# Pooled attention and experts on one core: the last two head pairs of a batch interleaved by row group, experts scaled and begun per row group, weight decoding in smaller tasks, and a new order

## The chip, the cores and the metric

The kernel runs on one core of a Trainium2 chip. The time is in device microseconds, from start to end of one execution, and a kernel's time is the median of its runs. TensorE is PE in the profile (its weight loads PEld), VectorE DVE, ScalarE ACT, GpSimd POOL, and SyncE, which issues all of this kernel's DMAs, SP.

## The reference

For 4 batches and 8 heads of 1152 keys with 64 values each, neighbouring queries are averaged in pairs (so 576 queries remain), attention is taken over all keys, and the result, 4 x 576 rows of 512 values, goes through two matrices with an exponential unit between them.

```python
q_pool = q.reshape(B, H, S // factor, factor, D).mean(axis=3)
scores = scale * np.matmul(q_pool, k.transpose(0, 1, 3, 2))
attn = softmax(scores)                      # with 1e-09 added to the sum
x = np.matmul(attn, v)                      # heads side by side: 2304 rows of 512
h = x @ w_in                                # 512 -> 2048
g = np.where(h > 0.0, h, np.exp(np.minimum(h, 0.0)) - 1.0)
return g @ w_out                            # 2048 -> 512
```

(The softmax is shortened here.) Everything is float32; the weights reach the kernel as 64-bit words, as the code's views of two 32-bit words show.

## The kernel before

**Arithmetic.** Every operand of a matmul is split into two float16 parts, a high half (the value scaled and rounded) and a low half (what is left). A product is then three matmuls or their equivalent. Making a low half is one VectorE instruction with two inputs in SBUF (`lo`, `plo`), or two instructions on POOL (a scaling and a subtraction).

**Attention.** Work goes batch by batch. A batch has 4 head pairs, and a pair has 9 steps: 4 tiles of 128 queries for each of its two heads, and one step with the last 64 queries of both. That is 144 steps in all. One step is: scores on PE (L643, L649) into the single PSUM buffer `s`; the maximum over the keys, which also moves the scores to SBUF, on DVE (L655); the exponential on ACT (L661), its sum (L666) and the reciprocal (L669); the high half of the probabilities on POOL (L672) or ACT (L680); the low half on DVE (L675), or, in the steps that the code calls slow, a scaling and a subtraction on POOL (L683 or L686 on ACT, L689); and a transposing DMA into `pT` (L699). Two steps share one product with the values on PE (L736, L742); ACT and DVE bring it into `x32` (L754, L759). The buffer `ep` holds a step's scores and probabilities from the maximum until the transpose has landed. There are 3 of these; batch 0 may also use the memory that w_out fills later (buffer names `wo`), and its `pT` the memory of `x16`.

**Before a pair begins**, `prep` loads q, k and v, adds the query pairs, finds the largest values by sums (L346), scales by them, makes the halves (L351 and L363 on ACT and DVE, or L306 and L369 on POOL), transposes keys and queries by DMA (L451, L439) and copies parts of the queries' transpose (L445, L448). `kT`, `qT` and `v16` have two buffers each.

**Weights.** `weights` loads each of 8 groups of both matrices in two halves, decodes the 64-bit words to float32 on DVE (L520, L524, L529), sums their sizes on ACT (L537), and makes halves once the scale is known (`split`: L574, L577, or L306 and L583 on POOL). Groups of w_in are scaled one by one, w_out as a whole.

**Experts.** When a batch's attention is complete, its largest value is found (L786, L793, then a turn on PE, L319 to L326), its rows are scaled into `x16` (L821 on ACT, L826 on DVE), and then come two row groups, rows 0 to 255 and rows 256 to 575: first matrix on PE (L850), the unit in five instructions on ACT, POOL and DVE (L858, L861, L866, L871, and the halves L885 to L897), and the second matrix on PE (L917, 12 matmuls a task), with the result scaled and written out (L928 to L938). `x16` has one buffer, and so has `x32`.

**What sets the order.** Nothing is scheduled on the chip. Each piece of work is a task with an engine, an assumed duration, a due time (`key`), what it follows, and the buffers that it uses; some have a second way on another engine. `Plan.run` places them one after another, on each free engine the ready task with the earliest due time whose buffers are free, and takes the second way where that ends sooner by its assumed durations (`WIN`, `PEN`). The instructions are then written in that order, and every engine runs its own in order. Due times are those of a step (`t0`, which advances by T0 or T1) shifted by a constant for each kind of work, all in `CFG`.

## Time and profile before

| | us |
|---|---|
| median of 3 runs | 980.82 |
| lowest and highest run | 978.5 and 980.83 |
| the profiled execution | 977.62 |
| its span, first to last instruction | 975.8 |
| PE busy | 745.6 (76%) |
| DVE busy | 747.6 (77%) |
| ACT busy | 627.9 (64%) |
| POOL busy | 519.0 (53%) |

No engine is busy all of the time; the shares are averages over stretches that differ. So the rows to look at are those by stretch, then the waits inside each, then single instructions in order of time. A row of instructions gives the line, the engine, the operation, what is written from what, shapes and count; behind the bar the busy time, the mean time of one in ns, and the idle time of the engine just before them with what ended it.

### The profile page before, as it was taken

Reading aid. Unit: us, or ns where it says so; the run is one execution under the profiler, and the core shown is the slowest. Engines: PE = TensorE matmul, PEld = TensorE weight load, DVE = VectorE, ACT = ScalarE, POOL = GpSimd, SP = SyncE. Lnnn points to the kernel's source line nnn. Section 1 sums busy time; section 2 is a strip of 40 time slices with the busy share of each in tenths; the row PEclk is TensorE's granted clock in tenths of the full one; section 3 lists DMA queues with packets and bytes.
Section 4 is the critical chain, followed back from the end, with each engine's and each line's share of the span. In section 5 each row is a group of like instructions: output and inputs, shape, how many; then the busy total and the mean of one; then the engine's idle time right before and its main releaser. Section 6 shows DMA issues by size and latency. Waiting matters only on the chain.

```text
span 975.8 us, 14669 instructions
## 1 busy us (share of the span) xinstructions
PE 745.6 (76%) x5271; PEld 416.6 (43%) x5271; DVE 747.6 (77%) x1200; ACT 627.9 (64%) x1093; POOL 519.0 (53%) x422
## 2 busy tenths in 40 slices
PE   0364464654258989889769997989698999999997
PEld 0122132322126645544346444544365455458563
DVE  5797989899789978788778776887877789845150
ACT  3576786666476868776557666865677778734260
POOL 4373867477579963783247634771276247505130
PEclk9998575556659999999979998999799999999999
DMA  7599899899956989999977989799888698640000
GB/s 238 134 212 228 190 199 254 184 227 222 271 109 126 177 156 184 171 177 184 183 148 137 206 163 193 132 203 190 172 174 172 132 176 135 123 94 7 22 2 27
DMA packets 434057, 156.94 MB, mean 161 GB/s; under 512 B 395840, under 2 KB 414272, under 8 KB 433984
## 3 DMA queue, kind: packets, MB, share of 16 engines
q1 hardware_dynamic: 433984, 156.01, 78.6%
q8 instruction: 41, 0.67, 0.3%
q14 instruction: 32, 0.26, 0.1%
HBM read 45.09 MB, written 4.72 MB: 51 GB/s over the span
## 4 chain that ended last, share of the span: by engine, by line
PE 32%; DMA 21%; DVE 12%; POOL 6%; issue 2%; ACT 2%; SPq 2%; DVEq 0%; POOLq 0%; ACTq 0%
DMA pT<-ep 16%; PE r L917 12%; PE r L850 8%; DVE ep L655 5%; PE r L736 4%; PE s L643 3%; DVE ep L675 3%; PE r L742 2%; PE s L649 2%; DMA kT<-kn 2%; DMA qT<-qn 1%; DMA q<-in_q_dram 1%; POOL ep L672 1%; ACT ep L661 1%; DVE tmp L871 1%
## 5 line engine op out<-in xcount | busy, mean ns | idle before, releaser
L655 DVE TENSOR_SCALAR_CACHE_REDUCE ep<-s,sm 128x1152 f32<-128x1152 f32 x133 | 188.0, 1414 | 80.1 <-DMA pT<-ep 52.2
L661 ACT ACTIVATE ep<-ep,nm 128x1152 f32<-128x1152 f32 x133 | 166.5, 1252 | 98.7 <-DVE ep L655 86.1
L850 PE MATMUL r<-x,wi 128*128 128x256 f16 (+1 forms) x1536 | 201.9, 290 | 9.3 <-DVE x L759 3.1
L643 PE MATMUL s<-kT,qT 128*128 128x512 f16 (+3 forms) x480 | 122.3, 370 | 113.1 <-DVE ep L655 88.9
L675 DVE SCALAR_TENSOR_TENSOR ep<-ep,nm 128x1152 f16<-128x1152 f32 x118 | 193.5, 1642 | 9.2 <-POOL ep L672 6.3
L917 PE MATMUL r<-wo,g 128*128 128x512 f16 (+1 forms) x864 | 174.8, 380 | 0.5 <-DVE tmp L871 0.3
L850 PEld LDWEIGHTS <-wi 128*128 128x128 f16 x1536 | 148.1, 99 | 60.1 <-issue 18.4
L736 PE MATMUL r<-pT,v 128*128 128x256 f16 (+1 forms) x864 | 100.8, 268 | 61.7 <-DMA pT<-ep 49.4
L672 POOL TENSOR_SCALAR ep<-ep,nm 128x1152 f16<-128x1152 f32 x52 | 73.2, 1408 | 104.2 <-DVE nm L669 102.5
L866 POOL TENSOR_SCALAR tmp<-tmp,us 128x320 f32<-128x320 f32 (+1 forms) x96 | 79.6, 830 | 90.4 <-ACT tmp L861 85.6
L680 ACT ACTIVATE ep<-ep,nm 128x1152 f16<-128x1152 f32 x81 | 101.3, 1251 | 31.0 <-DVE nm L669 30.7
L643 PEld LDWEIGHTS <-qT 128*128 128x128 f16 (+1 forms) x480 | 44.8, 106 | 174.8 <-issue 135.3
L917 PEld LDWEIGHTS <-g 128*128 128x128 f16 (+1 forms) x864 | 73.1, 100 | 88.9 <-issue 9.3
L736 PEld LDWEIGHTS <-v 128*128 128x128 f16 x864 | 68.8, 105 | 93.6 <-issue 47.7
L871 DVE SCALAR_TENSOR_TENSOR tmp<-r,wk,tmp 128x320 f32<-128x320 f32 (+1 forms) x96 | 58.0, 611 | 33.4 <-POOL tmp L866 33.2
L649 PE MATMUL s<-kT,qT 64*128 64x512 f16 (+3 forms) x480 | 80.8, 370 | 0.0
L754 ACT ACTIVATE x<-r,sm 64x256 f32<-64x256 f32 (+1 forms) x96 | 39.9, 415 | 47.3 <-PE r L742 45.4
L893 POOL TENSOR_SCALAR g<-tmp 128x320 f16<-128x320 f32 (+1 forms) x55 | 46.7, 850 | 35.8 <-DVE tmp L871 33.4
L742 PE MATMUL r<-pT,v 128*64 128x256 f16 (+1 forms) x864 | 65.5, 274 | 0.0
L858 ACT ACTIVATE tmp<-r 128x320 f32<-128x320 f32 (+1 forms) x96 | 46.3, 484 | 26.5 <-PE r L850 25.0
L889 POOL TENSOR_TENSOR g<-tmp,g 128x320 f16<-128x320 f32 (+1 forms) x54 | 56.8, 1058 | 4.8 <-ACT g L885 3.0
L861 ACT ACTIVATE tmp<-tmp,us 128x320 f32<-128x320 f32 (+1 forms) x96 | 57.7, 609 | 1.5
(136 smaller groups left out, 1029.2 us busy)
## 6 DMA issues: line engine op xcount, KB each, us to landing
k<-in_k_dram SPq DMA_DIRECT2D x16, 576.0 KB, 4.9
v<-in_v_dram SPq DMA_DIRECT2D x16, 576.0 KB, 4.9
q<-in_q_dram SPq DMA_DIRECT2D x32, 256.0 KB, 3.4
qT<-qT SPq DMA_DIRECT2D x48, 144.0 KB, 2.8
g<-in_moe_w_in_dram SPq DMA_DIRECT2D x13, 512.0 KB, 5.4
g<-in_moe_w_out_dram SPq DMA_DIRECT2D x13, 512.0 KB, 4.8
out_dram<-tmp SPq DMA_DIRECT2D x16, 256.0 KB, 2.5
pT<-ep SPq DMA_TRANSPOSE x133, 4.8
```

The costliest lines, as they stand in the source:

```text
L643: nc.tensor.matmul(s.ap[rows, c, 0:n], pr.qT.ap[:, 0, j, rows], keys[c], start=True, stop=False, skip_group_check=True,)
L649: nc.tensor.matmul(s.ap[rows, c, 0:n], pr.qT.ap[r, 1, j, rows], keys[c][r], start=False, stop=True, skip_group_check=True,)
L655: nc.vector.tensor_scalar(e_(), s.ap.rearrange("p a b -> p (a b)")[:, 0:S], pr.sm.ap[:, 12:13], None, op0=ALU.mult, op1=ALU.min, accum_out ...
L661: nc.scalar.activation(out=e_(), in_=e_(), func=AF.Exp, bias=nm.ap[:, 0:1], scale=-1.0, accum_out=nm.ap[:, 2:3],)
L672: nc.gpsimd.tensor_scalar(p_(0), e_(), nm.ap[:, 3:4], 1.0, op0=ALU.mult, op1=ALU.mult)
L675: nc.vector.scalar_tensor_tensor(out=p_(1), in0=e_(), scalar=nm.ap[:, 3:4], in1=p_(0), op0=ALU.mult, op1=ALU.subtract)
L680: nc.scalar.activation(out=p_(0), in_=e_(), func=AF.Copy, scale=nm.ap[:, 3:4])
L736: nc.tensor.matmul(x.ap[:, os], vt[:, order[c]].rearrange("p e d -> p (e d)"), pT.ap[:, c, cs], start=(c == 0), stop=False, skip_group_che ...
L742: nc.tensor.matmul(x.ap[r0:r0 + 64, os], vt[:, order[c], 0], pT.ap[:, NCH + c, cs], start=False, stop=(c >= NCH - 2), skip_group_check=True,)
L850: nc.tensor.matmul(hp.ap[:, f * n:(f + 1) * n], w[:, a, c, (f0 + f) * 128:(f0 + f + 1) * 128], x16.ap[:, e, c, g0:g0 + n], start=(i == 0), ...
L866: nc.gpsimd.tensor_scalar(en.ap[:, :m], en.ap[:, :m], -1.0, us.ap[:, 5:6], op0=ALU.add, op1=ALU.mult)
L917: nc.tensor.matmul(op.ap[r0:r0 + tn, :], gt[qd].ap[:, a, fi, o:o + tn], w_out16(f // 2)[:, e, f % 2, :], start=(i < 128 // tn), stop=(i >= ...
```

## The change

**Order of the steps.** The first two pairs of a batch keep their order. The last two are interleaved: the tiles 0 and 1 of both heads of pair 2, the same of pair 3, then the rest of pair 2 and the rest of pair 3. With the first half of this, rows 0 to 255 of the batch are complete; the time of it is kept in `u.ready`.

**Experts by row group.** `experts` is called once for each row group, with a start of its own. Each call finds the largest value of its own rows, scales them, and has its own scaling words (`us`, now 3 buffers); `x16` is shared by both calls of a batch.

**Weight decoding.** One task for two halves of a group becomes a task for each half, which waits for its own load alone, and also for the keys' low half of the very first pair (`first_keys`).

**Order made anew.** The constants are other ones, many of them apart for batch 0 (`K`); slow steps are every second of batch 0 as before, and every ninth after it (two in 36 to 39 before, and none behind that). The window in which a pair is prepared is set by PA and PB. `wm` has one buffer instead of two.

```diff
-            jobs = [(h, t) for h in range(2) for t in range(u.nt)] + ([(None, u.nt)] if u.lo else [])
+            mine.append(pr)
+        early = [(h, t) for h in range(2) for t in range(2)]
+        late_ = [(h, t) for h in range(2) for t in range(2, u.nt)] + [(None, u.nt)]
+        turns = [(pr, early + late_) for pr in mine[:-2]] + [(pr, early) for pr in mine[-2:]] + [(pr, late_) for pr in mine[-2:]]
+        for pr, jobs in turns:
...
+            if pr is mine[-1]:
+                u.ready.append(now)
...
-            prep(pr, prev.t0 - 2000.0, pr.t0 - 4000.0)
+            prep(pr, prev.t0 - CFG["PA"], pr.t0 - CFG["PB"])
+    first_keys = pairs[0].kl
...
-        td = plan.add("DVE", 4700.0, t0, dec, lds, raws + us + to)
-        tm = plan.add("ACT", 2 * act(512) + 260.0, t0, osum, [td], raws + us + to + wm)
+            td = plan.add("DVE", 2450.0, t0 + s, dec, [lds[s], first_keys], [raws[s], us[s]] + to)
+            tms.append(plan.add("ACT", act(512) + 130.0, t0 + s, osum, [td], [raws[s], us[s]] + to + wm))
...
-        slow = st.i < CFG["NS"] and st.i % PLM == PLM - 1
+        every = K("PLM", u)
+        slow = every and st.i % every == every - 1 and (u.i > 0 or st.i < CFG["NS0"])
...
-    def experts(u, t0, t1):
-        us, x16 = plan.buf("us"), plan.buf("x16")
+    def experts(u, gi, t0, t1):
+        us, x16 = plan.buf("us"), u.x16
+        g0, n = u.groups[gi]
...
-                    us.ap[:, to:to + 1], u.x32.ap[:, p0:p1, :u.n], axis=AX.XY, op=ALU.max, apply_absolute_value=True
+                    us.ap[:, to:to + 1], u.x32.ap[:, p0:p1, g0:g0 + n], axis=AX.XY, op=ALU.max, apply_absolute_value=True
...
-        if u.i + 1 < len(units):
-            experts(u, u.t1 + CFG["M0"], units[u.i + 1].t1 + CFG["M1"])
-        else:
-            experts(u, u.t1 + CFG["M0"], u.t1 + 100000.0)
+        u.x16 = plan.buf("x16")
+        ends = units[u.i + 1].ready if u.i + 1 < len(units) else [u.t1 + 100000.0, u.t1 + 200000.0]
+        experts(u, 0, u.ready[0] + CFG["M0"], u.ready[1] + CFG["M2"])
+        experts(u, 1, u.ready[1] + CFG["M2"], ends[0] + CFG["M1"])
```

The constants (`CFG`) are one line of numbers for another and are not shown. What they do to the order is shown at three places; a name there is a tile, and line numbers behind the change are its own.

The first is DVE at the start of the program, right behind the scaling words of the first pair (`sm`). `h` and `g` hold raw weights, `tmp` a decoder's scratch, and `qn`, `kn` and `v` the low halves of the first pair's queries, keys and values. Before:

```order
L306 TENSOR_SCALAR sm_94<-sm_94 128x1
L432 TENSOR_SCALAR sm_94<-sm_94 128x1
L520 TENSOR_SCALAR tmp_119<-h_91 128x512
L520 TENSOR_SCALAR tmp_120<-g_98 128x512
L524 SCALAR_TENSOR_TENSOR tmp_119<-h_91,tmp_119 128x512
L524 SCALAR_TENSOR_TENSOR tmp_120<-g_98,tmp_120 128x512
L529 SCALAR_TENSOR_TENSOR h_91<-h_91,tmp_119 128x512
L529 SCALAR_TENSOR_TENSOR g_98<-g_98,tmp_120 128x512
L363 SCALAR_TENSOR_TENSOR kn_96<-k_86,sm_94,kn_96 128x9x64 x2
```

After, at the same place:

```order
L324 TENSOR_SCALAR sm_94<-sm_94 128x1
L450 TENSOR_SCALAR sm_94<-sm_94 128x1
L381 SCALAR_TENSOR_TENSOR qn_93<-q_81,sm_94,qn_93 128x9x64
L381 SCALAR_TENSOR_TENSOR kn_96<-k_86,sm_94,kn_96 128x9x64 x2
L381 SCALAR_TENSOR_TENSOR v_123<-v_88,sm_94,v_123 128x18x64
L541 TENSOR_SCALAR tmp_136<-h_91 128x512
L542 SCALAR_TENSOR_TENSOR tmp_136<-h_91,tmp_136 128x512
L545 SCALAR_TENSOR_TENSOR h_91<-h_91,tmp_136 128x512
```

The keys' low halves stand ahead of the decoding instead of behind two halves of it, and the low halves of queries and values, which POOL made before, stand on DVE beside them.

The second is where the halves of w_out are made, at the change from batch 0 to batch 1. Before, on POOL (L306 and L583 on `wo` are one low half; L683, L689 and L672 belong to attention steps):

```order
L306 TENSOR_SCALAR wo_1325<-wo_1325,wk 128x512
L583 TENSOR_TENSOR wo_1325<-wo_1325 128x512
L689 TENSOR_TENSOR ep_1882<-ep_1882 128x1152
L306 TENSOR_SCALAR wo_1409<-wo_1409,wk 128x512
L583 TENSOR_TENSOR wo_1325<-wo_1409,wo_1325 128x512
L306 TENSOR_SCALAR wo_1409<-wo_1409,wk 128x512
L583 TENSOR_TENSOR wo_1325<-wo_1409,wo_1325 128x512
L683 TENSOR_SCALAR ep_1940<-ep_1940,nm_1939 128x1152
```

After, on DVE (L591 on `wo` is one low half, L669 a maximum, L689 a low half of probabilities):

```order
L591 SCALAR_TENSOR_TENSOR wo_1751<-wo_1751,wk 128x512 x2
L381 SCALAR_TENSOR_TENSOR v_2187<-v_1875,sm_1499,v_2187 128x18x64
L591 SCALAR_TENSOR_TENSOR wo_1751<-wo_1566,wk,wo_1751 128x512 x2
L689 SCALAR_TENSOR_TENSOR ep_2032<-ep_2032,nm_2031 128x1152
L591 SCALAR_TENSOR_TENSOR wo_1566<-wo_1566,wk 128x512 x2
L669 TENSOR_SCALAR ep_2277,nm_2276<-s_2178,sm_1130 128x1152
L591 SCALAR_TENSOR_TENSOR wo_1566<-wo_1320,wk,wo_1566 128x512 x2
L689 SCALAR_TENSOR_TENSOR ep_2127<-ep_2127,nm_2126 128x1152
L683 RECIPROCAL nm_2276<-nm_2276 128x1
L591 SCALAR_TENSOR_TENSOR wo_1320<-wo_1320,wk 128x512 x2
```

All 16 low halves of w_out stand on DVE after the change, where 6 stood on DVE and 10 on POOL.

The third is ACT in the last batch (`x_6424` is `x32`, `x_8313` is `x16`; L661 is a step's exponential, L754 an attention result, L928 an output). Before:

```order
L754 ACTIVATE x_6424<-r_8114,sm_6687 64x256
L661 ACTIVATE ep_8134,nm_8133<-ep_8134,nm_8133 128x1152
L666 ACTIVATE nm_8133<-nm_8133,wk 128x1
L928 ACTIVATE tmp_8166<-r_7973,us_5834 128x512
L754 ACTIVATE x_6424<-r_8171,sm_6687 64x256
L754 ACTIVATE x_6424<-r_8219,sm_6687 64x64 x2
L928 ACTIVATE tmp_8276<-r_8080,us_5834 128x512
L821 ACTIVATE x_8313<-x_6424,us_8060 128x4x256
L821 ACTIVATE x_8313<-x_6424,us_8060 128x4x320
```

After (L836 scales rows into `x16`, L675 is an exponential, L694 a high half of probabilities, L769 an attention result, L873 and L876 begin an expert tile's unit):

```order
L836 ACTIVATE x_8117<-x_6774,us_7932 128x4x256
L675 ACTIVATE ep_8115,nm_8114<-ep_8115,nm_8114 128x1152
L769 ACTIVATE x_6774<-r_8087,sm_6682 64x256
L680 ACTIVATE nm_8114<-nm_8114,wk 128x1
L694 ACTIVATE ep_8115<-ep_8115,nm_8114 128x1152
L873 ACTIVATE tmp_8192<-r_8132 128x512
L876 ACTIVATE tmp_8192<-tmp_8192,us_7932 128x512
L675 ACTIVATE ep_8164,nm_8163<-ep_8164,nm_8163 128x1152
...
L769 ACTIVATE x_6774<-r_8615,sm_7251 64x64 x2
L943 ACTIVATE tmp_8707<-r_8556,us_7932 128x512
L836 ACTIVATE x_8117<-x_6774,us_8438 128x4x320
```

The scaling of rows 0 to 255 and the units of their experts stand among the last steps, with six exponentials behind that scaling; only the 320 rows are scaled behind the last attention result.

## Rows read from the trace of the kernel before

**Rows 1.** Busy time by stretch: start:end, length, engines' busy us (count), PEclk, DMA share, GB/s

```profile
37.20:322.00 284.80, 155.84 (x956) 79.83 (x957) 255.99 (x420) 190.56 (x332) 194.94 (x112) 0.71 0.91 197
188.80:253.50 64.70, 33.42 (x191) 16.27 (x191) 59.66 (x94) 37.04 (x69) 40.97 (x23) 0.63 1.05 236
322.00:817.00 495.00, 433.79 (x3239) 245.20 (x3238) 399.18 (x626) 351.69 (x610) 263.43 (x238) 0.96 0.89 170
870.00:976.00 106.00, 100.86 (x674) 62.05 (x672) 34.53 (x65) 39.62 (x71) 24.28 (x35) 1.00 0.05 16
```

(The engines stand in the order PE, PEld, DVE, ACT, POOL.)

**Rows 2.** Waits of DVE, 322 to 817 us: total us, times, longest

```profile
DVE ep L655 <- DMA pT<-ep: 41.5, 32, 5.0
```

**Rows 3.** Timeline of PE from 868 us: start, us, what, count

```profile
869.30 0.34 PE L742 MATMUL r<-pT,v 128*64 128x64 f16 x9
...
876.81 21.17 PE L850 MATMUL r<-x,wi 128*128 128x256 f16 x192
897.82 5.34 PE L917 MATMUL r<-wo,h 128*128 128x512 f16 x24
903.00 15.70 PE L917 MATMUL r<-wo,g 128*128 128x512 f16 x72
918.54 26.30 PE L850 MATMUL r<-x,wi 128*128 128x320 f16 x192
944.67 26.18 PE L917 MATMUL r<-wo,g 128*128 128x512 f16 x144
```

**Rows 4.** Timeline of the start: DVE, SP's queue (SPq) and PE

```profile
13.87 1.39 DVE L520 TENSOR_SCALAR tmp<-h 128x512 uint32<-128x512 uint32 x1
...
20.41 4.78 DVE L363 SCALAR_TENSOR_TENSOR kn<-k,sm,kn 128x576 f16<-128x576 f32 x2
...
27.43 5.06 SPq L451 DMA_TRANSPOSE kT<-kn  x1
...
35.38 1.12 PE L643 MATMUL s<-kT,qT 128*128 128x512 f16 x3 [6.60 <-DMA qT<-qT]
```

**Rows 5.** Groups of instructions over the whole run, shapes kept apart

```profile
L675 DVE SCALAR_TENSOR_TENSOR ep<-ep,nm 128x1152 f16<-128x1152 f32 x118 | 193.5, 1642 | 9.2 <-POOL ep L672 6.3 <-ACT ep L680 2.6
L363 DVE SCALAR_TENSOR_TENSOR kn<-k,sm,kn 128x576 f16<-128x576 f32 x26 | 29.3, 1166 | 0.0
L369 POOL TENSOR_TENSOR v<-v,v 128x1152 f16<-128x1152 f32 x10 | 27.8, 2777 | 0.8
L871 DVE SCALAR_TENSOR_TENSOR tmp<-r,wk,tmp 128x512 f32<-128x512 f32 x32 | 23.8, 744 | 10.2 <-POOL tmp L866 10.0
L306 POOL TENSOR_SCALAR v<-v,sm 128x1152 f32<-128x1152 f32 x10 | 16.7, 1672 | 1.0 <-ACT v L351 0.6
L306 POOL TENSOR_SCALAR wo<-wo,wk 128x512 f32<-128x512 f32 x9 | 11.4, 1266 | 0.3 <-ACT wo L574 0.3
L577 DVE SCALAR_TENSOR_TENSOR wi<-g,wk,wi 128x512 f16<-128x512 f32 x11 | 10.3, 960 | 0.0
L363 DVE SCALAR_TENSOR_TENSOR v<-v,sm,v 128x1152 f16<-128x1152 f32 x6 | 9.3, 1546 | 1.9 <-POOL v L306 1.9
L363 DVE SCALAR_TENSOR_TENSOR qn<-q,sm,qn 128x576 f16<-128x576 f32 x5 | 5.5, 1104 | 0.0
```

**Rows 6.** A group of 37 to 322 us, and one line's shortest, median and longest ns

```profile
L675 DVE SCALAR_TENSOR_TENSOR ep<-ep,nm 128x1152 f16<-128x1152 f32 x18 | 37.7, 2093 | 0.1
...
L524 DVE SCALAR_TENSOR_TENSOR tmp<-g,tmp x26: 671/684/2847, 16.6 to 267.8; 128x512 uint32<-128x512 uint32 x26
```

**Rows 7.** A group of 37 to 322 us: idle time ahead of the maximum, and releasers

```profile
L655 DVE TENSOR_SCALAR_CACHE_REDUCE ep<-s,sm 128x1152 f32<-128x1152 f32 x34 | 48.0, 1411 | 18.7 <-PE s L649 9.5 <-DMA pT<-ep 8.6
```

**Rows 8.** DMA issues: count, us from issue to landing (median)

```profile
pT<-ep SPq DMA_TRANSPOSE x133, 4.8
qT<-qn SPq DMA_TRANSPOSE x16, 3.8
kT<-kn SPq DMA_TRANSPOSE x16, 5.8
```

127 lines of the change are left out of this document (65 added, 62 removed).

## Prediction

> **What bounds the kernel now.** I read the busy time by stretch first, then who waits, and last the single instructions at both ends of the program. The stretches [rows 1] cut the run at the 1st, 46th and 136th row maximum on VectorE (L655, one for each of the 144 attention steps) and at the end of the last attention product. Three different limits show. From 37 to 322 us (steps 1 to 45) DVE is busy 256.0 of 284.8 us, 90%, while PE is at 55% and its granted clock averages 0.71, so part of the stretch runs at 1.2 GHz and part at 2.4: DVE is the limit. From 322 to 817 us (steps 46 to 135) PE is busy 433.8 of 495 us (88%) and DVE 399.2 (81%); neither is full, and the longest wait of DVE there is for a transposed tile, 41.5 us [rows 2]: three `ep` buffers, each held until its transpose has landed, tie the engines together. After 870 us PE alone works: 100.9 of 106 us. In [rows 3] this tail is seen in a row: the last attention product at 869.30, some left-over expert work, then all of the last batch's experts, 21.2 + 5.3 + 15.7 + 26.3 + 26.2 us, with nothing beside them.
>
> The profiled execution took 977.6 us, 1.8 over its span of 975.8; the median of the three runs is 980.8, 3.2 above it. I make the sum as a difference against the profiled run and put it on the median.
>
> **The change, term by term.**
>
> *End.* With the last two pairs interleaved, rows 0 to 255 of the last batch are complete while steps are left. In the new order PE begins their experts behind the scores of step 140 of 144, and behind the last attention product stand 6 tasks of 12 output matmuls, then the 320-row experts. Now: 869.64 to 970.85 us, 101.2 us. After: 6 x 2.62 (15.70 / 72 x 12) + 26.3 + 26.2 = 68.2 us [rows 3], and a wait. The chain that must finish behind those six tasks (evacuation, maximum, turn, scaling) ran from 869.64 to 876.81 in the kernel before, 7.2 us with matmuls over it; the six tasks give it 15.7 us, but the return matmul stands only one task from the end of them, so I add 1.5 us for the two scaling instructions that follow it. That is 69.7, a gain of 31.5 us. Bounds: 24 (the chain is not covered) and 36 (part of the six tasks slips ahead of the last product). I take **-31**.
>
> *Start.* DVE now decodes two weight halves from 13.87 us, 6.5 us long, before the keys' low halves at 20.41; these take 4.8 us beside POOL, the next loads of k and v wait for them, and the transpose of the keys, issued at 27.43, occupies its queue for 5.06 us; the first scores follow at 35.38 [rows 4]. The new order puts low halves of q, k and v ahead of the decoding: 0.8 to 1.1 + 1.6 to 4.8 + 1.4 to 2.2 us, so keys are done 3 to 7 us sooner. But on SP the k and v loads now stand ahead of both transposes, and the row at 27.43 shows a transpose that sits in the queue while loads are under way, so about half is lost. **-3**, from -6 to +3.
>
> *Steps 1 to 45, the dear one.* Batch 0's experts start behind the scores of step 33 instead of 41, and the planner chose DVE over POOL more often. Counted in the order ahead of the 46th maximum, DVE gets 12 more low halves of w_out (x 0.960 = 11.5), 6 more of the keys (x 1.166 = 7.0), 4 more of v (x 1.546 = 6.2), 2 more of the probabilities (x 1.642 = 3.3), 7 more joins (x 0.744 = 5.2, a little high since 3 are narrower) [rows 5], and some 6 us of small ones (an estimate: two subtractions, a weight half, ten one-column instructions). Together +39 us on the engine that is the limit. POOL loses 5 pairs for v (1.672 + 2.777), 7 for w_out (two of 1.266) and 3 for keys (taken like those for v), about 53 us [rows 5], and 9 normalisations, and gets about 25 us of expert work earlier: net -40 of 195 us.
>
> That matters to DVE. The low half of the probabilities takes 2093 ns on average in this stretch against 1642 over the run [rows 5], and one and the same decode instruction ranges from 671 to 2847 ns with a median of 684 [rows 6]. Each group's time less its count times its shortest instruction, summed over this stretch's DVE groups (an estimate), is 50 us beside 195 us of POOL [rows 1], 0.26 us for each. So -40 of POOL gives back 10, and DVE's demand grows by 29 us.
>
> The Trainium skill's page "SBUF — State Buffer", section "Who interferes with whom", goes further: VectorE and GpSimd share a port pair by an exclusive lock, and the second to start waits until the first is done. The single worst rows agree (2847 against 671 ns); the mean, 0.26 us lost for one us of POOL, does not, since POOL mostly meets other instructions. By the rule taken in full, this term would be about -1 instead.
>
> Of the 29 us, what goes into DVE's idle 28.8 us? 9.5 us of it are waits for scores and 8.6 for transposes [rows 7]. The first should shrink, since earlier experts keep PE at the higher clock; in the densest piece, 188.8 to 253.5 us, DVE reached 92% [rows 1]. I take 13 us, a little under half of the idle time, as filled: **+16**. Bounds: +9 (DVE at 97%: 285 / 0.97 = 294) and +43 (39 us with no relief, at 90% busy).
>
> *Steps 46 to 135.* DVE loses 10 low halves of the probabilities (-16.4), which every ninth step now gives to ACT and POOL, and gets 4 for v (+6.2), 4 for q (+4.4), and about 8 us of scaling and subtractions, since each batch is scaled twice: +2. POOL is 36 us lighter, so DVE nets about -4 (36 x 0.16, this stretch's rate worked out in the same way, is 6). PE gets 15 us more expert work by the order. PE has 61 us of idle time here, DVE 96, and neither is full, so I let the two cancel: **0**. Bounds: -15 (DVE's waits for transposes, 41.5 us, fall by a third as steps follow each other more evenly) and +25 (PE's 15 as they are, and 10 for the mechanism of rival C).
>
> *Steps 136 to 144* keep their 53 us: PE loses 10 us of left-over experts, and DVE gets 12 of the new group's joins. The second buffer `wm` that is taken away (a scaling word of the weights) can delay a decode only behind the previous group's scaling; it lies in the second term.
>
> Sum: -31 - 3 + 16 + 0 = **-18**: 980.8 - 18 = 963 us.
>
> **Rivals.**
>
> *A, POOL was the brake.* If each us of POOL that goes was one that DVE waited for, the 40 us come back whole and the first 45 steps cost nothing (39 - 40). For it: the 2093 ns mean [rows 6]. Against: 0.26. -31 - 3 - 1 = -35: 980.8 - 35 = 946 us.
>
> *B, the first 45 steps stay bound by DVE and pay in full.* The place is the 285 us before the experts' main part; price +43, as above, because the idle time there is latency that the new order keeps. For it: 90% busy over all of the stretch, and 0.1 us of idle time ahead of the low halves [rows 6]. Against: POOL does get lighter. -31 - 3 + 43 = +9: 990 us, slower than before. It decides from +34 on, where it eats the whole gain of the two ends.
>
> *C, turnover of buffers.* kT, qT and v16 have two buffers each. Interleaved, the last two pairs hold both of each; pair 3 begins 4 steps after pair 2 (9 before), and the next batch's first pair has 5 steps between the release and its own scores. Into these must go transposes of 3.8 and 5.8 us and the copies that follow them, in one queue with the steps' own transposes of 4.8 us [rows 8]. Eight such turns at 2.5 us each: +20, so -18 + 20 = +2: 983 us, no change. Against: 4 steps are 22 us at 5.5 us a step, and no wait of PE for these tiles past the start is among the longer ones today.
>
> *D, it does not do what it says*: PE is in order, and an expert task placed too early would stall the scores behind it. It would look like C in time, and I give it no chance of its own.
>
> **How the numbers follow.** Forecast 0.42, A 0.20, B 0.24, C 0.14. The forecast's own range, from its middle bounds, is 948 to 978. A reaches down to 938 with the lower bound of steps 46 to 135 partly drawn; B reaches up to 994. Range 938 to 994. What a measurement of this kernel can tell from no change is 0.3%, 3 us. Faster: nearly all of the forecast and A, and a little of C: 0.64. Same: the forecast's edge and half of C: 0.10. Slower: B and the rest of C: 0.26.
>
> **What would show it.** End: from the last attention product to PE's end about 70 us, not 101. Start: first maximum near 34 us. First 45 steps: about 300 us long, DVE above 92%, the low halves' mean under 2.0 us; B would show 325 us, A 285 with means near 1.6. Steps 46 to 135: 495 us, PE above 90%; C would show waits of scores for kT or qT. The forecast is wrong if steps 46 to 135 move by more than 20 us either way, which no row here excludes.

## The result, and the profile after

The changed kernel takes 994.8 us (median; 993.0 to 998.7), 1.0148 times the kernel before, 95% interval 1.0109 to 1.0186: slower by 1.5%, clear of noise though under 2%. The forecast was 963 us, its range 938 to 994. The profiled execution spans 993.3 us, against 975.8 before. The first view to read is the busy time by stretch, cut at the 1st, 46th and 136th maximum (L669 now) and at the end of the last attention product. It answers [rows 1]. The columns are start:end, length, busy time of PE, PE weight loads, DVE, ACT and POOL, granted TensorE clock, DMA share and GB/s:

```profile
34.30:344.40 310.10, 198.17 (x1181) 102.52 (x1181) 279.46 (x471) 213.96 (x366) 143.74 (x93) 0.75 0.85 183
344.40:860.90 516.50, 441.89 (x3237) 247.52 (x3237) 396.18 (x653) 365.38 (x622) 230.48 (x215) 0.95 0.84 164
860.90:919.50 58.60, 52.96 (x442) 35.19 (x442) 38.91 (x66) 41.55 (x64) 24.98 (x22) 0.88 0.65 113
919.50:993.30 73.80, 68.41 (x411) 37.97 (x410) 20.78 (x47) 26.35 (x52) 11.63 (x20) 1.00 0.05 17
```

| stretch | before | after | difference | predicted |
|---|---|---|---|---|
| to the first maximum | 37.2 | 34.3 | -2.9 | -3 |
| steps 1 to 45 | 285.0 | 310.2 | +25.2 | +16 |
| steps 46 to 135 | 494.5 | 516.4 | +21.9 | 0 |
| steps 136 to the last product's end | 53.0 | 58.6 | +5.6 | 0 |
| from there to the end | 106.2 | 73.8 | -32.4 | -31 |
| span | 975.8 | 993.3 | +17.5 | -18 |

(The cut for steps 1 to 45 lies at 344.42.) Both ends of the program came out as forecast; the middle lost more than they gained.

Summed over steps 46 to 135, neither PE (442 us, 433 before) nor DVE (396, 399 before) has much more to do; in the sum, what grew is waiting. The sum hides where it happens. The stretch holds the first two pairs of batches 2 and 3 (steps 73 to 90 and 109 to 126). These take 24.9 us more, with 24.8 us more work on DVE and 23.7 on PE. The other steps have 27.3 us less work on DVE and are only 2.9 us shorter (288.1 for 291.0). The sums of the two windows of first pairs, before and after:

```profile
sum 203.46, PE 172.21 PEld 100.30 DVE 158.30 ACT 138.87 POOL 89.31; mean PE 86.11 PEld 50.15 DVE 79.15 ACT 69.44 POOL 44.66
sum 228.33, PE 195.95 PEld 108.73 DVE 183.06 ACT 164.40 POOL 122.86; mean PE 97.98 PEld 54.37 DVE 91.53 ACT 82.20 POOL 61.43
```

DVE's waits in all of steps 46 to 135, to be read against [rows 2] (what waits <- for what: us in total, times, longest):

```profile
DVE ep L669 <- DMA pT<-ep: 52.1, 32, 4.2
DVE nm L683 <- ACT nm L680: 20.1, 28, 2.2
DVE ep L689 <- POOL ep L686: 10.5, 9, 1.4
...
DVE x L774 <- ACT x L769: 9.1, 12, 1.8
```

PE's tail, beside [rows 3]: the last attention product (L757) ends at 919.47, six tasks of 12 output matmuls follow, and behind them the 320-row experts. PE waits 0.37 us in all of it for the scaled rows (L841). Columns: start, duration, instruction, count, idle time before it:

```profile
919.13 0.34 PE L757 MATMUL r<-pT,v 128*64 128x64 f16 x9
919.40 2.76 PE L932 MATMUL r<-wo,g 128*128 128x512 f16 x12
922.00 2.75 PE L932 MATMUL r<-wo,h 128*128 128x512 f16 x12
924.60 5.34 PE L932 MATMUL r<-wo,g 128*128 128x512 f16 x24
...
936.55 25.70 PE L865 MATMUL r<-x,wi 128*128 128x320 f16 x188 [0.37 <-DVE x L841]
962.09 26.18 PE L932 MATMUL r<-wo,g 128*128 128x512 f16 x144
```

The start, beside [rows 4]: the keys' low halves are done at 17.3 us, before any decoding, but their transpose is issued only at 21.84, behind two loads and the queries' transpose, and stands in its queue for 4.59 us. Its issue is 5.6 us earlier than in [rows 4], the first maximum 2.9, so half of the lead was lost, as the prediction had assumed. In both kernels the first scores wait last for a copy of the queries' transpose (`qT<-qT`, L466 now), which stands behind both transposes in the queue; it is issued 2.7 us earlier (30.01 for 32.74):

```profile
15.79 1.54 DVE L381 SCALAR_TENSOR_TENSOR kn<-k,sm,kn 128x576 f16<-128x576 f32 x2
...
19.20 2.57 SPq L457 DMA_TRANSPOSE qT<-qn  x1
...
21.84 4.59 SPq L469 DMA_TRANSPOSE kT<-kn  x1
...
30.01 0.46 SPq L466 DMA_DIRECT2D qT<-qT  x1
...
32.46 1.12 PE L657 MATMUL s<-kT,qT 128*128 128x512 f16 x3 [0.79 <-DMA qT<-qT]
...
34.27 1.42 DVE L669 TENSOR_SCALAR_CACHE_REDUCE ep<-s,sm 128x1152 f32<-128x1152 f32 x1 [5.08 <-PE s L663]
```

### The profile page after: what moved, and what is told of

It is laid out like the page before. It is cut to its first block, busy times and chain, and to the rows that moved or that the text cites. A ratio compares the mean times of both kernels' runs of the same rounds, so it can differ in the third digit from the quotient of the medians.

```text
span 993.3 us, 14724 instructions
## 1 busy us (share of the span) xinstructions
PE 765.5 (77%) x5283; PEld 425.0 (43%) x5283; DVE 751.7 (76%) x1269; ACT 658.6 (66%) x1122; POOL 414.4 (42%) x357
## 4 chain that ended last, share of the span: by engine, by line
PE 34%; DMA 18%; DVE 14%; POOL 6%; issue 4%; ACT 3%; SPq 1%; DVEq 0%; POOLq 0%; ACTq 0%
DMA pT<-ep 16%; PE r L932 13%; PE r L865 7%; DVE ep L669 5%; PE r L751 4%; PE s L657 4%; PE s L663 3%; PE r L757 2%; DVE ep L689 2%; DMA q<-in_q_dram 1%; POOL tmp L881 1%; ACT ep L675 1%; POOL g L904 1%; DVE tmp L886 1%; DVE tmp L542 1%
## 5 line engine op out<-in xcount | busy, mean ns | idle before, releaser
L669 DVE TENSOR_SCALAR_CACHE_REDUCE ep<-s,sm 128x1152 f32<-128x1152 f32 x136 | 192.1, 1413 | 76.3 <-DMA pT<-ep 57.1
L675 ACT ACTIVATE ep<-ep,nm 128x1152 f32<-128x1152 f32 x136 | 170.2, 1251 | 102.1 <-DVE ep L669 93.2
L865 PE MATMUL r<-x,wi 128*128 128x256 f16 (+1 forms) x1536 | 199.4, 288 | 2.6 <-DVE tmp L886 1.4
L932 PE MATMUL r<-wo,g 128*128 128x512 f16 (+1 forms) x888 | 182.5, 383 | 2.2 <-DVE tmp L886 2.2
L689 DVE SCALAR_TENSOR_TENSOR ep<-ep,nm 128x1152 f16<-128x1152 f32 x110 | 165.1, 1501 | 15.2 <-POOL ep L686 11.9
L865 PEld LDWEIGHTS <-wi 128*128 128x128 f16 x1536 | 147.5, 98 | 49.8 <-issue 11.2
L694 ACT ACTIVATE ep<-ep,nm 128x1152 f16<-128x1152 f32 x95 | 118.8, 1250 | 28.5 <-DVE nm L683 28.0
L751 PE MATMUL r<-pT,v 128*128 128x256 f16 (+1 forms) x846 | 106.5, 281 | 33.6 <-DMA pT<-ep 24.8
L881 POOL TENSOR_SCALAR tmp<-tmp,us 128x320 f32<-128x320 f32 (+1 forms) x96 | 75.1, 784 | 103.1 <-ACT tmp L876 98.4
L932 PEld LDWEIGHTS <-g 128*128 128x128 f16 (+1 forms) x888 | 77.3, 101 | 92.1 <-issue 9.6
L686 POOL TENSOR_SCALAR ep<-ep,nm 128x1152 f16<-128x1152 f32 x41 | 53.2, 1298 | 141.4 <-DVE nm L683 139.8
L703 POOL TENSOR_TENSOR ep<-ep 128x1152 f16<-128x1152 f32 x26 | 67.8, 2607 | 55.5 <-ACT ep L700 49.2
L904 POOL TENSOR_TENSOR g<-tmp,g 128x320 f16<-128x320 f32 (+1 forms) x54 | 62.4, 1162 | 16.9 <-ACT g L900 16.0
L769 ACT ACTIVATE x<-r,sm 64x256 f32<-64x256 f32 (+1 forms) x96 | 39.9, 416 | 41.0 <-PE r L757 39.7
L757 PE MATMUL r<-pT,v 128*64 128x256 f16 (+1 forms) x846 | 65.1, 277 | 0.0
L873 ACT ACTIVATE tmp<-r 128x320 f32<-128x320 f32 (+1 forms) x96 | 46.5, 484 | 23.7 <-PE r L865 19.2
L876 ACT ACTIVATE tmp<-tmp,us 128x320 f32<-128x320 f32 (+1 forms) x96 | 57.1, 609 | 1.5
```

What stands on the lines that cost most here:

```text
L669: nc.vector.tensor_scalar(e_(), s.ap.rearrange("p a b -> p (a b)")[:, 0:S], pr.sm.ap[:, 12:13], None, op0=ALU.mult, op1=ALU.min, accum_out ...
L675: nc.scalar.activation(out=e_(), in_=e_(), func=AF.Exp, bias=nm.ap[:, 0:1], scale=-1.0, accum_out=nm.ap[:, 2:3],)
L689: nc.vector.scalar_tensor_tensor(out=p_(1), in0=e_(), scalar=nm.ap[:, 3:4], in1=p_(0), op0=ALU.mult, op1=ALU.subtract)
L694: nc.scalar.activation(out=p_(0), in_=e_(), func=AF.Copy, scale=nm.ap[:, 3:4])
L751: nc.tensor.matmul(x.ap[:, os], vt[:, order[c]].rearrange("p e d -> p (e d)"), pT.ap[:, c, cs], start=(c == 0), stop=False, skip_group_che ...
L757: nc.tensor.matmul(x.ap[r0:r0 + 64, os], vt[:, order[c], 0], pT.ap[:, NCH + c, cs], start=False, stop=(c >= NCH - 2), skip_group_check=True,)
```

## The experiments

Two questions were open: why steps 46 to 135 grew, and what the first 45 steps paid for. The ratio of each kernel below is to the kernel before, with its 95% interval; the times of stretches come from one profiled execution each. Single profiles differ: i2 below keeps DVE's order of before up to the 61st maximum, and still its steps 1 to 45 took 288.3 us instead of 285.0. So a difference of 3 us in a stretch is no finding.

### Which part of the change: constants, slow steps, halves, last batch

**e1, the changed code with the constants of before** (`us` with two buffers).

```diff
-    LOADS=70959, ..., KM=-3090, KE=104873, ..., KE0=162320, ..., PLM=9, M2=13636, ..., PB=12759,
+    LOADS=39538, PLM=0, ..., KM=7701, KE=39223, ..., KE0=39223, ..., PB=4000, M2=32900
```

> The changed code with the constants of the kernel before (the slow steps of batch 0 alone, the old windows, the old pacing of the experts moved 22.8 us of due time ahead for the earlier start). Theory 1: the 22 us lost in steps 46 to 135 come from the structure, the interleaving and the two scalings a batch; then this run loses them too (about 515 us there) and ends near 990. Theory 2: they come from the new constants (every ninth step slow, other due times); then steps 46 to 135 take about 495 us here and the whole is near 970. In both the last product to the end should be near 74 us, since the tail hangs on the structure alone, and the first 45 steps show whether the extra DVE work there is the planner's choice under the new constants (then 285 us) or the earlier experts' (then 305).

Measured 1006.2 us, 1.0278 [1.0241, 1.0314]. Steps 1 to 45 take 290.0 us, steps 46 to 135 535.3, the rest 142.8. So all but 5 us of the 25 lost in the first 45 steps come with the new constants, which begin batch 0's experts sooner; what they buy is at the end (132.4 instead of 142.8) and in between (516 instead of 535). Over steps 1 to 135 the two kernels take the same time, 825.3 and 826.6 us: the constants move the loss and do not make it. The tail behind the last attention product is 87.2 us here, not the 74 expected, so it does not hang on the structure alone.

**e5, no slow steps behind batch 0**: in the order of the changed kernel, POOL's and ACT's part of them is an ordinary low half on DVE.

```diff
+        if slow and u.i > 0:
+            norm_pool = norm_act = lambda: None
+            plo_pool = plo
```

> The changed kernel in its own order, with one edit: the slow steps of batches 1 to 3 (every ninth) make their low half by one VectorE instruction at the place where POOL's subtraction stood, and the normalisation on ACT or POOL is dropped. Theory 2a: the slow steps hold an ep buffer longer and cost the waits that grew (POOL's high half, 4.9 to 10.5 us; the transposes, 41.5 to 52.1); then steps 46 to 135 shrink by 10 us or more. Rival: they relieve DVE as meant; then the stretch grows by up to 14 us, 10 times 1.4. If neither binds there, within 3 us.

Measured 997.1 us, 1.0185 [1.0110, 1.0261]; steps 46 to 135 take 516.1 us (516.4 with them). In this stretch the slow steps neither cost nor help.

**e6, low halves given back to POOL**, all but one instruction of them in the first 45 steps: 10 of w_out, 5 of v, 3 of keys, at their place in the changed order. (The cut shows w_out alone.)

```diff
+            if which and (g, s) not in ((0, 0), (1, 0), (2, 0), (4, 0), (5, 0), (7, 0)):
+                t.back = lo_pool
```

> The changed kernel in its own order, with 10 low halves of w_out, 5 of v and 3 of the keys in batches 0 and 1 given back to POOL at the same places, as the kernel before had them. If DVE's added instructions are what makes the first 45 steps 25 us longer, these 18 (about 10 x 0.96 + 5 x 1.55 + 3 x 2.33 = 24 us, less 10 for POOL's interference) shorten the stretch from 310 by about 14 us. If POOL's interference weighs as much as the instructions themselves, or the earlier experts and not these halves are the cost, nothing is gained, or it grows.

Measured 1012.2 us, 1.0339 [1.0297, 1.0381]. Steps 1 to 45, the first of its windows here, are 14 us longer, though DVE does 6 us less in them:

```profile
35.20:359.30 324.10, 196.81 (x1181) 101.22 (x1182) 273.14 (x451) 214.17 (x366) 186.86 (x127) 0.76 0.80 175
```

The expected gain did not come. At this place in the order the halves are better on DVE. What DVE's added work costs by itself this run can't tell, since POOL became 43 us busier and other work waits for it.

**e3, the kernel before with only the last batch interleaved and done by row group**, and the experts of the batch before it paced 22.8 us of due time faster, to make room.

```diff
+        if u.i == B - 1:
+            turns = [(pr, plain) for pr in mine[:-2]] + [(pr, early) for pr in mine[-2:]] + [(pr, late_) for pr in mine[-2:]]
```

> The kernel before with one part of the change and only in the last batch: its last two pairs interleaved, its two row groups scaled and begun apart, and the experts of the batch before it paced 22.8 us of due time faster to make room. If the tail is won by that alone, the last product to the end is 74 us against 106, and what the faster pacing costs shows in steps 100 to 144: at no cost the whole ends near 950, if PE has to pay for each us of expert work that is moved ahead of the last product (some 30 us), near 980.

Measured 989.6 us, 1.0108 [1.0079, 1.0137]. The tail is as short as in the changed kernel, but the nine steps ahead of it take 85.4 us instead of 53.0:

```profile
828.80:914.20 85.40, 84.02 (x640) 51.09 (x640) 46.99 (x77) 43.14 (x76) 30.60 (x32) 1.00 0.44 82
914.20:987.90 73.70, 65.23 (x399) 36.36 (x395) 23.34 (x49) 26.87 (x55) 8.96 (x17) 0.98 0.06 19
```

159.1 us in all, as before (159.2). PE is busy for 84.0 of the 85.4 us, and in the tail it waits for some 3.5 us until its last matmul, so what was moved in front of the last product only came sooner. The changed kernel gains 26.8 us there because less expert work is left: PE's expert matmuls behind the 136th maximum are 48.2 + 47.7 us, and were 60.0 + 74.5. The work went into the first 45 steps, where they are 32.6 + 23.8 us; in the kernel before 16.5 and none. The rows by stretch (PE, PE weight loads, clock) for the first matrix alone (L865) in the changed kernel:

```profile
34.30:344.40 310.10, 32.60 (x252) 25.20 (x252) 0.75 0.85 183
...
860.90:993.30 132.40, 48.22 (x384) 37.21 (x384) 0.95 0.32 59
```

And for the second matrix (L932):

```profile
34.30:344.40 310.10, 23.81 (x96) 9.84 (x96) 0.75 0.85 183
...
860.90:993.30 132.40, 47.70 (x240) 21.20 (x240) 0.95 0.32 59
```

### Which resource sets the length of steps 46 to 135

**f1 and f2, a third of the expert matmuls left out**, in the changed kernel and in the kernel before, orders kept.

```diff
-                            terms = [(a, e, c) for a, e in ((0, 0), (0, 1), (1, 0)) for c in range(KD)]
+                            terms = [(a, e, c) for a, e in ((0, 0), (1, 0)) for c in range(KD)]
```

> The changed kernel, same order of every engine, with 8 of every 12 expert matmuls (the terms with one of the low halves are left out), so that TensorE has about 80 us less to do in steps 46 to 135. Beside the same cut in the kernel before: the two stretches differ by 22 us uncut. If TensorE's experts standing in front of scores make the difference, it falls below 7 us with the cut. If it is on VectorE and its chain of steps, it stays at 18 to 26 us. If TensorE binds at all there, each stretch falls by over 40 us; if steps wait for VectorE and for transposes, by under 20.

> The kernel before, same order, with 8 of every 12 expert matmuls (the terms with one of the low halves are left out). Steps 46 to 135 take 494.5 us uncut. If TensorE binds there, under 455 us; if VectorE and the transposes bind, over 475.

f1: 981.8 us, 1.0010 [0.9982, 1.0038]; f2: 952.5 us, 0.9718 [0.9678, 0.9757]. The stretch (columns as above) in f1:

```profile
343.50:863.20 519.70, 391.03 (x2729) 207.17 (x2729) 394.93 (x653) 365.86 (x623) 230.37 (x215) 0.89 0.83 162
```

And in f2:

```profile
321.60:812.20 490.60, 379.25 (x2720) 201.85 (x2719) 402.21 (x626) 352.56 (x610) 263.50 (x238) 0.92 0.89 171
```

PE has some 50 us less to do in each (80 were expected; the granted clock was 0.89 and 0.92 here, 0.95 and 0.96 without the cut), and the stretch moves by +3 and -4 us. PE's 88% were no limit. The two stretches differ by 29 us with the cut and by 22 without it, so experts that stand in front of scores on PE don't make the difference. (Within f1 the first two pairs of batches 2 and 3 became 7 us shorter, and the other steps 10 us longer.) Nearly all of the gain is in the tail (60.5 us in f1, 73.8 without the cut; 87.4 in f2, 106.2 without).

**d1 and d2, cheaper low halves of q, k and v on DVE**, from the fifth pair on: they are made zero by an instruction with one input, and so left out of the result.

```diff
+                if pr.i >= 4:
+                    for o, i, m in pairs_:
+                        ts(nc.vector, o, m, 0.0, 1.0)
+                    return
```

> The changed kernel, same order. From the fifth pair on VectorE's low halves of q, k and v are replaced by a multiplication of the high half by zero (one input instead of two), so these low parts are left out of the result. In steps 46 to 135 VectorE makes 34 of them: 20 (27.5 us) in the first two pairs of batches 2 and 3 (steps 73 to 90 and 109 to 126), 14 (17.0 us) in the other stretches, where the interleaved pairs are. Theory floor: the first two pairs of a batch are bound by VectorE's work, the interleaved ones by the three ep buffers, whatever VectorE has to do. Then the first two pairs lose nearly all that is saved, 15 to 22 us of their 228, and the others under 5 us of their 288. Rival, VectorE's work counts alike everywhere: 15 to 22 and 9 to 13 us. Rival, it counts nowhere and waits grow instead: under 6 us in all.

> The same cut in the kernel before (low halves of q, k and v on VectorE, from the fifth pair on, replaced by a multiplication by zero, and so left out of the result). There VectorE makes 7 of them (9.5 us) in steps 73 to 90 and 109 to 126 and 19 (21.5 us) in the other stretches of steps 46 to 135. Theory floor: 494.5 us fall by 8 to 14, less than in the changed kernel, since its pairs stand near the floor of the ep buffers already. If VectorE's work counts alike everywhere: by 18 to 25.

d1: 982.5 us, 1.0031 [1.0009, 1.0054]; d2: 975.4 us, 0.9955 [0.9934, 0.9977]. DVE's busy time in the stretch falls by 22.1 us in d1 (to 374.1) and 17.8 in d2 (to 380.9); the stretch falls by 7.8 (to 508.6) and 0.5 (to 494.0). Most of what DVE no longer does turns into waiting. (The profiled execution of d1 is the slowest of its seven, 3.9 us over their median, so the gain there may be larger.) In d1 the first two pairs of batches 2 and 3 lose 6.6 us of 13 us less work, the others 1.2 of 9: the theory floor has the places right and more than half of the size wrong. At this rate, 0.5 us of time for 1 us of work, the 24.8 us of added DVE work in those pairs would make some 12 of the 25 us that they lost (an estimate). In d2 the floor theory is wrong in size too: 0.5 us for the 8 to 14 expected.

**g1, the same low halves moved to POOL** in steps 37 to 54, 73 to 81 and 109 to 117 of the changed kernel.

```diff
+            if t.eng == "DVE" and "lo.<locals>.f" in t.emit.__qualname__ and (n - 1) // 9 in (4, 5, 8, 12) and "POOL" in t.ways:
+                t.emit = t.ways["POOL"][1]
```

> The changed kernel, same order of all else; the low halves of q, k and v that VectorE makes in steps 37 to 54, 73 to 81 and 109 to 117 are made by GpSimd at the same place (GpSimd is 26 and 32% busy in the last two). Theory floor: steps 73 to 81 and 109 to 117, 60.5 and 58.0 us long with 46 us of VectorE work, lose 4 to 7 us each; in the early stretch, where GpSimd is slower at it and others wait for it, between -4 and +6. In all 985 us, 978 to 995. If VectorE's work is not what these steps wait for: 995 or more.

Measured 1014.5 us, 1.0377 [1.0318, 1.0436]: steps 46 to 135 take 530.4 us, with 10 us less on DVE. Steps 73 to 81 and 109 to 117 became 1.5 and 3.0 us longer instead of 4 to 7 shorter. The expectation missed. It does not refute the theory that the uneven load of DVE between the pairs costs time, since POOL got 29 us more work in exchange for DVE's 10; it shows that POOL is no place for it.

**c1 and c2, only the high half of the probabilities transposed and used**, in both kernels.

```diff
-                out=pT.ap[:, :, half * 128:half * 128 + 128], in_=ep.ap[:, 0:2 * S]
+                out=pT.ap[:, 0:NCH, half * 128:half * 128 + 128], in_=ep.ap[:, 0:S]
```

> The changed kernel, same order; the transposing DMA of a step takes the high half of the probabilities alone, and the product with the values leaves the low half out. VectorE still makes the low half. The transpose, 2.8 us or more, becomes shorter, and with it the time that a step holds one of the three ep buffers (15.6 us). Theory floor: if it is shorter by 1.2 us, a step in the interleaved pairs is shorter by a third of that, so the 288 us of steps 46 to 72, 91 to 108 and 127 to 135 fall by 15 to 30 us, and the 228 us of the batches' first two pairs by under 8. If VectorE's own order of instructions is what holds the steps, both fall by under 6.

> The kernel before, same order, with only the high half of the probabilities transposed and used (the low half is left out of the product), as in c1_after_high_only, where steps 46 to 135 went from 516.4 to 479.5 us. If the hold of the three ep buffers limits both kernels alike, 494.5 falls by 30 to 42 here. If it limits the changed one alone, by under 15.

c1: 939.2 us, 0.9589 [0.9545, 0.9633]; c2: 917.5 us, 0.9372 [0.9332, 0.9411]. The stretch falls by 36.9 us (to 479.5) and by 40.8 (to 453.7), and DVE's wait for transposes almost goes. In c1:

```profile
DVE ep L669 <- DMA pT<-ep: 6.7, 6, 1.9
```

And in c2:

```profile
DVE ep L655 <- DMA pT<-ep: 5.7, 6, 2.4
```

Of what was relieved here (PE, DVE, and the turn of a step through one of the three `ep` buffers), the turn is the one that both kernels answer to. Three things changed with it: the transfer became shorter, from 5.2 to 3.8 us on average from issue to landing; it no longer waits for the low half; and PE's product is shorter, by 27 and 34 us in all, which f1 and f2 show to be worth little. The first two pairs of batches 2 and 3, for which c1's expectation had under 8 us, fell by 16.1, the other steps by 20.9. The turn limits both kernels alike, so it says where the length is made, but not why the changed one is longer.

### The structure, or any other order

Counted over the rows of maxima and landings of steps 46 to 135 (90 of each), a step of the changed kernel holds its buffer, from the maximum to the landing, 15.67 us (15.56 before), but from a landing to the next maximum that may use the buffer pass 1.51 us on average (0.85). Hold and gap, summed and divided by three buffers, are the stretch: 470 + 45 us after, 467 + 26 before. (That is a way of counting, and by itself shows no cause.) In c1 hold is 12.03 us and gap 3.90, in c2 11.69 and 3.39: of 3.6 and 3.9 us less hold, the whole turn keeps 1.25 and 1.33, close to the 1.43 and 1.35 by which the transfer is shorter. The rest came back as gap, part of it the low half, which now stands behind the landing.

**h1 and h2, maxima written ahead on DVE**, in both kernels: a maximum passes the expert joins and the low halves that stand right before it.

```diff
+        crossed = ("join", "gl_dve", "lo", "xmax")
...
-        for t in self.run():
+        for t in self.hoisted(self.run()):
```

> The changed kernel; on VectorE, from step 37 to step 136, a step's maximum is written ahead of the expert joins, expert low halves and low halves of q, k and v that stand right before it and that it does not depend on: it passes 20 joins, 5 expert low halves and 11 tasks of prepared pairs. All else is in the same order. Counted over steps 46 to 135, a step holds its ep buffer 15.67 us (15.56 before the change), but from the landing that frees a buffer to the next maximum 1.51 us pass (0.85 before), and VectorE is busy with other instructions in nearly all of that. Theory order: these instructions stand ahead of the maximum by the order alone; then the 516 us fall by 8 to 15, and the joins and low halves take idle time behind it. Rival: what is passed delays the step before it by as much (its low half, its reciprocal), the hold grows as the gap shrinks, and the stretch stays within 4 us of 516.

> The kernel before with the same passing of maxima: 19 tasks passed. Here the gap is 0.85 us a step, 25.6 us of the 494.5 in all (a third of the sum, for three buffers). Theory order: the stretch falls by 2 to 6 us. Rival: within 2 us.

h1: 1012.9 us, 1.0350 [1.0308, 1.0392]; h2: 988.4 us, 1.0090 [1.0055, 1.0125]. Steps 46 to 135 grew to 532.3 and 501.6 us. In h1 hold is 16.13 us and gap 1.57. DVE's idle part of the gap grew from 8.2 to 13.5 us (summed, divided by three), and its wait for scores ahead of a maximum from 9.3 to 24.1: a maximum that stands ahead of its time makes the rest wait. The instructions in the gap filled it; taking them out did not shorten it. Both theories had it wrong, the second by less.

**e4, the kernel before with the small decoding tasks alone.**

```diff
-        td = plan.add("DVE", 4700.0, t0, dec, lds, raws + us + to)
+            td = plan.add("DVE", 2450.0, t0 + s, dec, [lds[s], first_keys], [raws[s], us[s]] + to)
```

> The kernel before, its constants, with the weight decoding in smaller tasks behind the first pair's keys alone, and one buffer wm. By the prediction's term for the start, the first maximum comes 3 us sooner (34.2 instead of 37.2) and the rest stays: 978 us. If a new order by itself costs something, as the other kernels that were planned anew show, steps 46 to 135 take 500 to 510 us instead of 494.5, and the time is 983 to 992.

Measured 992.9 us, 1.0136 [1.0101, 1.0171]. The first maximum is at 35.2 us, steps 1 to 45 take 267.8, steps 46 to 135 530.1: weight work moved behind the 46th maximum, but the sum of both, 797.9, is 18.4 above the 779.5 of before.

**e7 and e8, one half of the structure each**, with the constants of before. e7 is e3 with the interleaving in every batch; its experts are done by row group in the last batch alone. e8 is the changed code, small decoding included, without interleaving in batches 0 to 2. The first cut is against e3, the second against the changed code.

```diff
-        if u.i == B - 1:
+        if True:
             turns = [(pr, plain) for pr in mine[:-2]] + [(pr, early) for pr in mine[-2:]] + [(pr, late_) for pr in mine[-2:]]
```

```diff
+        if u.i < B - 1:
+            turns = [(pr, early + late_) for pr in mine[:-1]] + [(mine[-1], early), (mine[-1], late_)]
```

> The kernel before with its own constants, the last two pairs of every batch interleaved, but the experts of batches 0 to 2 scaled and begun as a whole; the last batch by row group. It belongs beside e3_last_only, which has the same experts and interleaves the last batch alone (steps 46 to 135: 508 us, VectorE idle 96 us of it), and beside e1_old_constants, which has both parts in every batch (535 us, idle 119). If the interleaving brings VectorE's extra idle time (more buffers held, next pairs prepared in fewer steps), idle is 115 to 120 us here and the stretch 525 to 535 us. If the row groups bring it (two scalings, the first group's experts due in fewer steps), idle stays at 95 to 100 us and the stretch at 505 to 512.

> The changed code with the constants of before and without interleaving in batches 0 to 2: the row groups alone. The first group is then complete five steps before the batch ends. If the row groups bring VectorE's extra idle time in steps 46 to 135, it is 115 to 120 us here and the stretch 525 to 535 us; if the interleaving does, idle is 95 to 100 us and the stretch 505 to 512.

e7: 1016.3 us, 1.0368 [1.0328, 1.0409]; e8: 1003.0 us, 1.0232 [1.0203, 1.0262]. Steps 46 to 135 take 526.9 and 538.6 us, with 113 and 121 us of DVE idle. The two had been set against each other, and both show their sign: each of the two costs about what both together cost in e1.

**i1 and i2, the kernel before with one constant moved**, the end of the experts' due times by 0.8 us later and 1.2 us sooner.

```diff
-..., M0=8135, M1=33164, KS=15043, ...
+..., M0=8135, M1=34000, KS=15043, ...
```

> The kernel before with one constant changed: the experts' due times end 0.8 us later (M1 34000 instead of 33164). No structure is changed; VectorE's order is the old one up to the 59th maximum, and 175 of its 785 tasks stand elsewhere behind it. If an order planned anew costs by itself in steps 46 to 135, whatever it was made for, they take 500 to 520 us instead of 494.5, and the time is 984 to 1000. If the loss belongs to the changed structure (interleaving, row groups), they stay at 492 to 498 us, and the time at 977 to 983.

> As i1_pace_later, with the experts' due times ending 1.2 us sooner (M1 32000); 114 of VectorE's 785 tasks stand elsewhere, from the 61st maximum on, and a little less expert work is left for the end. If a new order costs by itself: 500 to 520 us in steps 46 to 135. If not: 492 to 498, and 975 to 981 us in all.

i1: 990.3 us, 1.0115 [1.0082, 1.0149]; i2: 994.4 us, 1.0161 [1.0127, 1.0194], as much as the whole change. Nothing but the order differs. i2 in steps 46 to 135, beside the second row of [rows 1]: the same work, 9.8 us more time.

```profile
326.00:830.30 504.30, 440.15 (x3251) 248.50 (x3249) 399.06 (x627) 357.58 (x613) 270.06 (x244) 0.96 0.88 167
```

Put together over steps 1 to 135, so that work which crosses the 46th maximum doesn't count twice (us, sums of the two windows):

| kernel | what differs from before | steps 1 to 135 | DVE busy | DVE idle | from step 136 |
|---|---|---|---|---|---|
| before | | 779.5 | 654.9 | 124.6 | 159.2 |
| i1, i2 | one constant | 788.5, 792.6 | 655.2, 653.9 | 133.3, 138.7 | 161.1, 161.5 |
| h2 | 19 tasks passed | 791.6 | 653.7 | 137.9 | 158.8 |
| e3 | structure in the last batch only | 791.5 | 656.8 | 134.7 | 159.1 |
| e4 | small decoding | 797.9 | 666.0 | 131.9 | 159.5 |
| e7 | interleaving in every batch | 822.9 | 668.3 | 154.6 | 155.6 |
| e8 | row groups in every batch, small decoding | 825.8 | 674.2 | 151.6 | 140.7 |
| e1 | both, small decoding | 825.3 | 679.7 | 145.6 | 142.8 |
| after | both, small decoding, new constants | 826.6 | 675.6 | 151.0 | 132.4 |

Five other orders of nearly the same work cost 9 to 18 us, nearly all of it as DVE idle time where DVE's work is unchanged. (i2's 13.1 includes the 3.3 us of steps 1 to 45, where its order is that of before; its median is 15.3 us longer all the same.) The four with either half of the structure in every batch cost 43 to 47: 13 to 25 us more DVE work and 21 to 30 us more idle. The cleanest pair is e7 and e3, which differ by the interleaving of batches 0 to 2: 31 us. e8 can be set beside e4, which has the small decoding too: 28 us. No kernel here that does the whole computation beats the kernel before.

The count of hold and gap puts the growth of steps 46 to 135 at different places: hold is 16.25 us in e4, 16.42 in e7, 16.65 in e1, 16.81 in e8, and the gaps there are 1.1 to 1.5; in the changed kernel nearly all of it is in the gap. No one part of the turn is what a new order lengthens.

## Why the prediction was wrong

**End, right in its size, incomplete in its account.** -32.4 for -31: six tasks, and no wait worth naming. But e3 shows that this gain is none by itself: where PE is full on both sides of the last product, work moved ahead of it is paid in front of it. The changed kernel gains because expert work went into the first 45 steps.

**Start, right.** -2.9 for -3, by the mechanism named: low halves sooner, and both transposes behind the loads of k and v in their queue. What the first scores waited for last was the copy behind the transposes, which the prediction's term did not name.

**Steps 1 to 45: +25 for +16. The step that failed is "13 us, a little under half of the idle time, as filled".** DVE's work grew by 23 us (279.5 for 256.2; +29 predicted), and its idle time did not shrink (30.6 us, 28.8 before): 90% busy both times, so rival B's mechanism held, with less than its price. The waits for scores and transposes of [rows 7] did go down, from 18.1 to 7.8 us, but others took their place; DVE's largest wait there is now for ACT's half of an attention result, 10.7 us against 4.3:

```profile
DVE x L774 <- ACT x L769: 10.7, 8, 3.5
DVE ep L669 <- PE s L663: 6.0, 2, 5.1
...
DVE ep L669 <- DMA pT<-ep: 1.8, 3, 1.1
```

The relief from POOL was real: the low half takes 1.60 us on average in this stretch, where [rows 6] has 2.09. If 39 us of work were added and 23 us are measured, 51 us of POOL less gave back 16, 0.31 us for each (0.26 in the prediction). e6 is the same the other way round: halves worth 24 us by [rows 5] went from DVE to POOL (10 x 0.960 + 5 x 1.546 + 6 x 1.166), DVE became only 6 us lighter, and POOL 43 heavier: 0.42. Both figures are high, because the mean times of [rows 5] already hold time that was lost beside POOL. Counted at each instruction's shortest time (an estimate), the added work is 32 us and the relief 10, and both pairs of kernels give 0.2. The Trainium skill's page "SBUF — State Buffer", section "Who interferes with whom", has the one that comes second wait for the whole instruction of the first, but among VectorE's instructions it counts those with two inputs in SBUF, and of the others only those in its 2-port modes. So it states no price of 1 for every us of POOL, as the prediction read it, and an average of 0.2 over a mixed stream does not contradict it.

**Steps 46 to 135: +22 for 0. The step that failed is "I let the two cancel".** It weighed busy times summed over the stretch, 15 us more for PE against 4 us less for DVE (measured: 9 more and 3 less). Some 50 us taken off PE moved the stretch by 4 us at most (f1, f2), and 18 to 22 taken off DVE by 0.5 to 8 (d1, d2), so such sums don't price it. Nor do they cancel where they fall: DVE's work went up by 24.8 us in the first two pairs of batches 2 and 3, which became 24.9 us longer, and down by 27.3 in the other steps, which gave back 2.9. The prediction had named what does count, the three `ep` buffers, and then costed the term by something else. It also kept the length of a finely fitted order for a new one; the runs i1 and i2 price that at 8 to 10 us here. The time itself, +21.9, lies within the term's own upper bound of 25, but for another reason; it is beyond the 20 us that the prediction had set as its sign of being wrong.

**Rival C** had the size (+20) and not the mechanism: PE has no wait for `kT` or `qT` among its longer ones in this stretch. Its largest is for the maximum that frees the scores' buffer, 54.0 us where the kernel before has 35.0:

```profile
PE s L657 <- DVE ep L669: 54.0, 31, 4.9
PE r L751 <- DMA pT<-ep: 9.4, 12, 1.5
```

**Rival B** said 990 us, near the 994.8 measured, and that is luck: its price of 43 was 25, and the 22 us of steps 46 to 135, which it had at nothing, made up for it.

**Rival A** is out: POOL is 51 us lighter in the first stretch, and 25 us were lost there. **Rival D** finds no support: with a third of the expert matmuls gone from both kernels their stretches differ by more, not less (f1, f2). **Steps 136 to 144: +5.6 for 0**: in the nine steps PE does experts of the last batch for part of the time in which it did those of the batch before, at a granted clock of 0.88 (1.00 before).

**What stays open.** That the interleaving of batches 0 to 2 costs 31 us (e7 against e3), and that e8's row groups stand 28 us over e4, is measured; why is not. DVE has 13 to 25 us more work in these kernels, and 21 to 30 us more idle time that is not traced to one cause. The place of the maxima (h1) and PE (f1) are excluded as the main one, as far as these runs moved them. Uneven load of DVE fits the places of the loss, and d1's rate would give it about half of the 25 us of steps 46 to 135; that it is the cause is argued, not shown, since no run here evens the load without loading another engine. Nor is it shown what makes the order of before fit so well.

## What to carry to other kernels

Where several in-order engines share a ring of few buffers, cost a stretch by the whole turn of a buffer, hold and gap together, and not by the engines' busy shares: work taken off an engine at 88% may give nothing, and a shorter hold counts only as far as the turn shortens (here 1.3 of 3.6 to 3.9 us). Before letting two sums cancel, ask in which steps each of them falls. Where an order was searched out over many constants, count a toll for any new order before the change's own terms; here 9 to 18 us of 980. And when work moves out of a tail, ask which stretch takes it in: a tail that shrinks by 32 us gains nothing if the engine becomes full in front of it as well.
